# Small matmuls in column and row tiles, two thirds of an inverse transform, wider loads and a delayed output projection in an attention and FFT-gate kernel

## The chip, the cores and the metric

The kernel runs on one core of one Trainium2 chip. TensorE (PE) multiplies matrices into PSUM, VectorE (DVE) and ScalarE (ACT) do the elementwise work, GpSimd (POOL) adds a few tensors and starts most loads, and SyncE (SP) starts the stores. The metric is the time of one execution on the device in microseconds (us). "Span" is the part of it that the profile covers, about 2 us less. "Clock" is the mean share of full speed that TensorE was granted. Each run has a state, fast or slow; only fast runs are compared here.

## The reference, cut to what matters

```python
kv  = einsum('bhsd,bhse->bhde', k, v)        # 8 batches, 8 heads, 576 positions, 64 per head
o   = einsum('bhsd,bhde->bhse', q, kv)
o   = o / sqrt(mean(o*o, -1) + 1e-6) * g_norm
x   = o.transpose(0, 2, 1, 3).reshape(8, 576, 512)
x1, x2, x3 = split(x @ w_proj, 3, axis=-1)   # 512 -> 3 * 512
y   = x1 * irfft(rfft(x2, axis=1) * rfft(filter_fft, axis=0)) * x3   # along the 576 positions
out = y @ w_out                              # float32, 8 x 576 x 512
```

## The kernel before

Everything is held with channels on the 128 partitions and positions in the free dimension, until the x2 projection turns it. The transform over 576 positions is split into three groups of frequencies (those divisible by three, and the rest), so that x is first folded: with thirds x_0, x_1, x_2 it makes `rr = x_0 + x_1 + x_2` and `ab = (x_0 - x_2, x_1 - x_2)`. A batch's attention is computed between the stages of the batch before it, so that TensorE always has something to do.

```python
def att_x(b, j):                  # x = o * rstd, four times per batch
    ...
    bc = ps_tile("ps_bc")
    for h in range(2):            # spread rstd of each head over its 64 partitions
        nc.tensor.matmul(bc[:, h, 0:TH], ind_bc[:, j], s['rstd'][:, h], start=True, stop=True)
    nc.vector.tensor_mul(out=s['x'][:, j].rearrange("p (a b) -> p a b", a=2), in0=bc[:, :, 0:TH],
                         in1=s['o'][:, j].rearrange("p (a b) -> p a b", a=2))

def inv(b, dc):                   # all three thirds of the inverse transform
    ...
    for g in range(2, 6):
        nc.tensor.matmul(ip[:, 0:2, 0:SB], Y[:, g, d_], IV[:, g, 0:2 * SB].rearrange("p (a b) -> p a b", a=2), ...)
        nc.tensor.matmul(ip[:, 2, 0:SB], Y[:, g, d_], IV[:, g, 2 * SB:S], ...)
    nc.vector.tensor_add(out=u, in0=ip[:, 0:3, 0:SB], in1=st[b]['cs'][:, dc].to_broadcast([P, 3, SB]))
    nc.vector.tensor_mul(out=st[b]['yg'][:, dc], in0=u.rearrange("p a b -> p (a b)"), in1=g13[:, dc])

for b in range(B):
    proj2(b); kv(b + 1); qtr(b + 1); fft(b)
    load_kv(b + 2); load_q(b + 2)
    for dc in range(4):
        proj13(b, dc); att_o(b + 1, dc)
    invc(b)
    att_r(b + 1)                  # row sums and rstd
    for dc in range(4):
        inv(b, dc); att_x(b + 1, dc)
    fold(b + 1)
    outp(b)                       # output projection
# cut: the tests whether there is a next batch
```

The whole kernel:

## Time and profile before

| | before |
|---|---|
| time, median of 4 runs | 299.94 us (299.25 to 300.9) |
| span of the profiled run | 297.9 us, of which 44.6 before the first x2 projection and 29.9 after the start of the last |
| steady batch, start to start of the x2 projection | 31.9 us |
| granted clock in the steady batches | 1.00 |

TensorE is busy 87% of the span, its clock is granted in full in all slices after the prologue's, and it carries two thirds of the chain: it is the bottleneck. The table of stretches shows two steady batches; its columns are the window with its length, then busy us of PE, of PE's weight loads, of DVE, ACT and POOL, each with its count, then the granted clock, the share of the DMA engines, and GB/s.

```profile
108.50:140.40 31.90, 30.61 (x221) 18.68 (x223) 18.93 (x26) 15.17 (x24) 14.63 (x14) 1.00 0.86 94
140.40:172.30 31.90, 30.61 (x221) 18.65 (x223) 18.94 (x26) 15.16 (x24) 14.63 (x14) 1.00 0.85 94
```

Of 31.9 us TensorE works 30.61 and DVE 18.94. The last lines come from the chain that ended last, through the second half of the second batch: start, us, and what.

```profile
...
159.52 0.65 ACT sq L213
...
162.13 0.69 ACT rstd L226
...
162.87 0.40 PE ps_bc L234 x2
...
172.33 0.75 PE ps_x L286 x3
```

From 159.52 to 162.82 the chain is on ScalarE, from the square to rstd. TensorE isn't idle for that long: its timeline shows a wait of 0.56 us for rstd, before the broadcasts at 162.87.

### The profile page before, as it was taken

How to read it: one execution, taken by the hardware profiler on the slowest of the kernel's cores; microseconds unless marked ns; L12 is line 12 of the kernel's file. 1: busy time of each engine (PE TensorE's matmuls, PEld its weight loads, DVE VectorE, ACT ScalarE, POOL GpSimd, SP SyncE). 2: the span in 40 equal slices, each digit the busy share in tenths (PEclk: the TensorE clock that was granted, in tenths of full speed). 3: DMA queues.
4: the chain of work that ended last, by engine and by line, in shares of the span. 5: the costliest groups of instructions: out<-in, count | busy, mean ns of one | idle time of the engine just before them, and what ended most of it. 6: DMA issues, size and time to landing. Idle time of an engine off the chain costs nothing.

```text
span 297.9 us, 4540 instructions
## 1 busy us (share of the span) xinstructions
PE 260.5 (87%) x1816; PEld 158.6 (53%) x1833; DVE 175.0 (59%) x272; ACT 131.6 (44%) x197; POOL 124.2 (42%) x131
## 2 busy tenths in 40 slices
PE   0128699999999999999999999999999999999992
PEld 0027346664567436754666455744775367644760
DVE  7993431939184745657383909382756547482760
ACT  1135435380637243753457073815274336614313
POOL 8874568890099006920395019800240006000600
PEclk9999779999999999999999999999999999999999
DMA  5999999999499639990699049934000220004004
GB/s 34 151 189 206 172 126 152 112 104 71 161 87 112 42 134 79 124 64 27 150 144 78 2 158 115 105 21 161 0 3 0 81 80 0 3 0 158 2 0 158
DMA packets 95415, 26.58 MB, mean 89 GB/s; under 512 B 79970, under 2 KB 90786, under 8 KB 95394
## 3 DMA queue, kind: packets, MB, share of 16 engines
q0 software_dynamic: 90272, 16.85, 69.3%
q1 hardware_dynamic: 5122, 9.44, 8.9%
q8 instruction: 14, 0.23, 0.3%
q14 instruction: 7, 0.06, 0.1%
HBM read 33.69 MB, written 9.44 MB: 145 GB/s over the span
## 4 chain that ended last, share of the span: by engine, by line
PE 66%; DVE 19%; ACT 10%; issue 4%; ACTq 0%; DVEq 0%
PE ps_x L319 17%; PE ps_out L359 12%; PE ps_x L286 12%; PE ps_inv L343 6%; DVE tpw L302 5%; PE ps_bc L234 4%; DVE qT L203 3%; DVE tpw L303 3%; PE ps_kv L186 3%; PE ps_inv L345 2%; ACT osb L214 2%; PE ps_h L262 2%; ACT sq L213 2%; PE ps_qT L202 2%; PE ps_o L212 2%
## 5 line engine op out<-in xcount | busy, mean ns | idle before, releaser
L319 PE MATMUL ps_x<-x,wp 128*128 128x288 bf16 x512 | 67.5, 286 | 4.4 <-DVE tpw L303 4.4
L304 POOL TENSOR_TENSOR Y<-tpw 97x1024 bf16<-97x1024 f32 (+1 forms) x16 | 38.0, 2381 | 74.8 <-DVE tpw L303 74.8
L319 PEld LDWEIGHTS <-wp 128*128 128x128 bf16 x512 | 50.0, 98 | 19.7 <-issue 5.7
L107 POOL DMA_DIRECT2D kb<-in_k_dram x32 | 28.5, 903 | 73.3 <-PE ps_kv L187 67.3
L361 ACT COPY ot<-ps_out 128x1024 f32<-128x1024 f32 (+1 forms) x24 | 20.0, 867 | 63.7 <-PE ps_out L359 63.1
L203 DVE COPY qT<-ps_qT 128x1152 bf16<-128x1152 bf16 x16 | 11.5, 753 | 52.3 <-PE ps_qT L202 52.3
L325 DVE TENSOR_TENSOR g<-ps_x,x 128x576 bf16<-128x576 f32 x32 | 24.0, 754 | 25.7 <-PE ps_x L319 25.7
L359 PE MATMUL ps_out<-wo,yg 128*128 128x512 bf16 (+1 forms) x152 | 38.2, 383 | 0.4
L323 ACT CAST x<-ps_x 128x576 bf16<-128x576 f32 x32 | 20.4, 639 | 39.7 <-PE ps_x L319 39.7
L115 POOL DMA_DIRECT2D qb<-in_q_dram x40 | 34.0, 879 | 2.1 <-DMA wo<-in_moe_w_out_dram 1.8
L347 DVE TENSOR_TENSOR u<-ps_inv,cs 128x576 bf16<-128x576 f32 x32 | 24.0, 753 | 17.0 <-PE ps_inv L345 17.0
L343 PE MATMUL ps_inv<-IV,Y 128*128 128x384 bf16 x128 | 34.0, 328 | 0.0
L345 PE MATMUL ps_inv<-IV,Y 128*128 128x192 bf16 x128 | 31.4, 246 | 0.0
L235 DVE TENSOR_TENSOR x<-ps_bc,osb 128x576 bf16<-128x576 f32 x32 | 23.7, 749 | 7.1 <-PE ps_bc L234 6.2
L213 ACT ACTIVATE sq<-ps_o 128x576 bf16<-128x576 f32 x32 | 20.9, 652 | 15.4 <-PE ps_o L212 15.4
L359 PEld LDWEIGHTS <-yg 128*128 128x128 bf16 (+1 forms) x160 | 14.0, 100 | 23.9 <-issue 8.4
L288 ACT CAST x<-ps_x 128x1024 bf16<-128x1024 f32 (+1 forms) x24 | 20.1, 872 | 11.2 <-PE ps_x L286 11.2
L214 ACT ACTIVATE osb<-ps_o,g_col 128x576 bf16<-128x576 f32 x32 | 23.6, 738 | 0.0
L302 DVE TENSOR_TENSOR tpw<-ps_X,HH 97x1024 f32<-97x1024 f32 (+1 forms) x16 | 19.5, 1219 | 6.8 <-PE ps_X L300 6.3
L286 PE MATMUL ps_x<-wp,ab 128*128 128x512 bf16 x96 | 22.0, 379 | 0.0
L173 PE MATMUL ps_ft<-ident,IV 128*128 128x128 bf16 (+1 forms) x25 | 3.7, 306 | 18.9 <-ACT IV L163 18.3
L343 PEld LDWEIGHTS <-Y 128*128 128x128 bf16 x128 | 12.5, 97 | 13.1 <-issue 6.7
(91 smaller groups left out, 355.0 us busy)
## 6 DMA issues: line engine op xcount, KB each, us to landing
out_dram<-ot SPq DMA_DIRECT2D x16, 512.0 KB, 3.1
kb<-in_k_dram POOLq DMA_DIRECT2D x32, 128.0 KB, 4.6
vb<-in_v_dram POOLq DMA_DIRECT2D x8, 512.0 KB, 6.8
qb<-in_q_dram POOLq DMA_DIRECT2D x32, 128.0 KB, 5.8
wp<-in_moe_w_proj_dram POOLq DMA_DIRECT2D x3, 512.0 KB, 10.5
out_dram<-ot SPq DMA_DIRECT2D x8, 128.0 KB, 3.1
kt<-in_k_dram POOLq DMA_DIRECT2D x8, 64.0 KB, 4.0
vt<-in_v_dram POOLq DMA_DIRECT2D x8, 64.0 KB, 5.8
```

The lines of the kernel that those rows point to most:

```text
L107: nc.gpsimd.dma_start(out=kb[i][:, c], in_=src4(k, c * D, [1, D]))
L115: nc.gpsimd.dma_start(out=qb[b % 2][:n, c], in_=q[b, :, c * P:c * P + n, :].transpose([1, 0, 2]))
L213: nc.scalar.activation(out=s['sq'][:, j].rearrange("p (a b) -> p a b", a=2), in_=op[:, :, 0:TH], func=AF.Square)
L214: nc.scalar.activation(out=s['o'][:, j].rearrange("p (a b) -> p a b", a=2), in_=op[:, :, 0:TH], func=AF.Copy, scale=g_col)
L286: nc.tensor.matmul(pp[:, cc], t[:, j, o * P:(o + 1) * P], wp[:, j, DM:2 * DM], start=(j == 0), stop=(j == NDC - 1))
L302: nc.vector.tensor_mul(out=t_[:n, 0], in0=xp[:n], in1=HH[:n, g, 1:3])
L304: nc.gpsimd.tensor_add(out=Y[:n, 2 * g:2 * g + 2], in0=t_[:n, :, 0], in1=t_[:n, :, 1])
L319: nc.tensor.matmul(pp[:, h, 0:TH], w_, x[:, j, h * TH:(h + 1) * TH], start=(j == 0), stop=(j == NDC - 1))
L325: nc.vector.tensor_mul(out=st[b]['g13'][:, dc].rearrange("p (a b) -> p a b", a=2), in0=pp[:, :, 0:TH], in1=x1)
L343: nc.tensor.matmul(ip[:, 0:2, 0:SB], Y[:, g, d_], IV[:, g, 0:2 * SB].rearrange("p (a b) -> p a b", a=2), start=(g == 2), stop=(g == 5))
L345: nc.tensor.matmul(ip[:, 2, 0:SB], Y[:, g, d_], IV[:, g, 2 * SB:S], start=(g == 2), stop=(g == 5))
L359: nc.tensor.matmul(pp[:m, cc], yg[:, dc, c * P:c * P + m], wo[:, dc], start=(dc == 0), stop=(dc == NDC - 1))
```

## The change

The change wants to take work off TensorE, and waits out of its way:

- k^T v, the q transposes, the row sums, and the tails of the x2 and output projections have half-width or narrower outputs. They are put side by side in column tiles, two or four matmuls on the array at once: in the trace of before the 20 column-tiled filter matmuls of 512 columns follow each other at 0.114 us, full ones at 0.22. The broadcasts have short contractions and go in row tiles: eight take 0.45 us on the chain of the changed kernel, where two took 0.40 before.
- The three thirds of that part of the inverse which comes from frequencies not divisible by three sum to zero. So only two thirds of it are computed, and DVE makes the last from them.
- k is loaded in pieces of 1 KB, as v was before, and q in pieces of 2304 bytes (nine positions of one head side by side, in float32), both instead of 256 bytes. In q, position 9t + c then lies at row t, and the transposes give the positions ordered by c, then t. Something must bring them back into order, and the x multiply does it while it writes.
- The filter is folded as x is; three passes instead of six make the tables.
- The output projection of a batch runs in the next batch, between the row sums and the broadcasts.

The diff is cut to its core:

```diff
-            nc.gpsimd.dma_start(out=qb[b % 2][:n, c], in_=q[b, :, c * P:c * P + n, :].transpose([1, 0, 2]))
+            nc.gpsimd.dma_start(out=qb[b % 2][64 * g:64 * g + 64],
+                in_=bass.AP(tensor=q.tensor, offset=..., ap=[[NR * D, 64], [S * D, 4], [1, NR * D]]))   # NR = 9
 ... # kv: pairs of heads in column tiles
+                    nc.tensor.matmul(kvp[64 * hp:64 * hp + 64, 0, j * D:(j + 1) * D], kk, vv, ...)
 ... # att_x
-        nc.vector.tensor_mul(out=s['x'][:, j].rearrange("p (a b) -> p a b", a=2), in0=bc[:, :, 0:TH],
-                             in1=s['o'][:, j].rearrange("p (a b) -> p a b", a=2))
+            nc.vector.tensor_mul(out=s['x'][:, j].rearrange("p (h t c) -> p h c t", h=2, c=NR),
+                                 in0=bc[i][:, :, 0:TH].rearrange("p h (c t) -> p h c t", c=NR),
+                                 in1=s['o'][:, j].rearrange("p (h c t) -> p h c t", h=2, c=NR))
 ... # inv: 16 matmuls of 384 columns, and the last third from the first two
+                nc.tensor.matmul(ip[:, i, 0:2 * SB], Y[:, g, d_], IV[:, g, 0:2 * SB], ...)
+        nc.vector.tensor_add(out=u[:, :, 0:2], in0=pq, in1=cs.to_broadcast([P, 2, 2, SB]))
+        nc.vector.tensor_sub(out=w_, in0=cs[:, :, 0], in1=pq[:, :, 0])
+        nc.vector.tensor_sub(out=u[:, :, 2], in0=w_, in1=pq[:, :, 1])
 ... # the loop over the batches
-        invc(b)
         if nxt:
             att_r(b + 1)
-        for dc in range(NDC):
-            inv(b, dc)
-            if nxt:
-                att_x(b + 1, dc)
+        if b:
+            outp(b - 1)
         if nxt:
+            att_x(b + 1, 0)
+            att_x(b + 1, 1)
             fold(b + 1)
-        outp(b)
+        invc(b)
+        for dp in range(2):
+            inv(b, dp)
+    outp(B - 1)
```

In the new x multiply, the innermost index of the output, t, moves by nine elements of bf16: every element is written 18 bytes after the one before it.

## The prediction

> **What bounds the kernel now.** The page shows a 297.9 us span with PE busy 87%, DVE 59%, ACT 44%, POOL 42%. The table of stretches shows a steady batch of 31.9 us holding 30.6 us of PE, 18.9 of DVE and 15.2 of ACT. Starts in the PE timeline give each stage's cost per batch: x2 projection 4.42 us, k^T v 1.11, q transposes 1.12, transform 2.8, x1/x3 projection 7.84, attention product 0.98, row sums 1.08, broadcasts 1.4, inverse 3.93 plus 0.66, output projection 4.39: about 29.8 us. The other 2.1 us is waits: 0.63 for the spectrum multiplies, 0.56 for rstd. Before the loop, 44.7 us pass: six DVE table passes until about 22 us, an ACT-bound attention stage to 33.5, filter matmuls to 44.7, some at 0.43 us each on a slow clock.
>
> **What changes per batch, on PE.** Inverse: 16 matmuls of 384 columns at 0.163 us instead of 384+192 at 0.246: -1.3. Output tail, shared by two batches: -0.5. Tail of the folded x2 projection, in halves: -0.4. Row sums, four column tiles: about -0.5. Broadcasts in row tiles: about -0.8. That column tiles overlap is already shown: the 20 half-width filter matmuls of 512 columns took 2.28 us, 0.114 each, against 0.22 for full ones. k^T v becomes 40 matmuls of 64 columns and the transposes 36; [...] weight loads last 98 ns at 128 columns, 125 at 97, 110 at 64. I estimate 3.1 us for both stages, from 2.2: +0.9. Sum: PE about 27.2 us.
>
> **On DVE.** Rebuilding the third third costs about +0.8 us of busy time, the split q copies +0.3. DVE rises to about 20 us. The x multiplies now write at an 18-byte step; I expect them to stay near 0.75 us.
>
> **Critical path.** Output projection one batch behind hides the rstd wait. But x multiplies and fold (about 4.7 us on DVE) now stand before the next x2 projection, covered by 3.3 us of inverse: a new wait of about 0.5-0.9 us for the folded x. Broadcasts wait about 0.5 us for PSUM. The wait before the x1/x3 projection stays, 0.5-1 us. So about 2 us of waits stay, and DVE is almost co-critical. Batch: about 29.2 us, not 27.2; saved over the loop, some 19 us.
>
> **Prologue.** Three table passes instead of six (-8 us), 1 KB instead of 256 B reads, 22 instead of 40 filter matmuls, DVE sharing the first attention stage. DVE must wait for the filter load before the first q copies, so I take -10 us: first x2 projection near 34-35 us. The end grows by about 3.5 us (one more output projection), which batch 0 loses.
>
> **Predicted time: 271 us, 8 in 10 within 260 to 284.** Chances: faster 0.94, within 2% 0.04, slower 0.02.
>
> **Right or wrong is shown by:** steady batch 28.5-30 us in the stretches; inverse near 2.6 us; k^T v plus transposes 2.5-3.5 us; the x2 projection waiting on DVE's fold; x multiplies near 0.75 us; first x2 projection at 33-37 us.
>
> **What would make it wrong.** Narrow weight loads not overlapping: +1.5 us a batch. Stretched x multiplies [...]: up to +2.5 us a batch. A late filter load: +5 us. Fewer waits than I count: -1.5 us a batch.

Two passages are cut from this text. 29.8 us of TensorE's stages, less 1.3, 0.5, 0.4, 0.5 and 0.8, plus 0.9, is 27.2. But the +0.9 (3.1 from the measured 2.2) is only the author's estimate, set beside three measured weight-load times, the -0.8 for row tiles is an estimate too (the trace of before has none), and the "up to +2.5 us", outside the sum, has no measured duration behind it.

## More of the kernel before

Lines of the page of the kernel before follow: busy times of the engines with their shares of the span, TensorE's granted clock in tenths in 40 slices of the span, the engines' shares of the chain that ended last, and one group of instructions (line, engine, operation, tiles, shapes, count, then busy us and mean ns of one, then idle time before them).

```profile
PE 260.5 (87%) x1816; PEld 158.6 (53%) x1833; DVE 175.0 (59%) x272; ACT 131.6 (44%) x197; POOL 124.2 (42%) x131
...
PEclk9999779999999999999999999999999999999999
...
PE 66%; DVE 19%; ACT 10%; issue 4%; ACTq 0%; DVEq 0%
...
L235 DVE TENSOR_TENSOR x<-ps_bc,osb 128x576 bf16<-128x576 f32 x32 | 23.7, 749 | 7.1 <-PE ps_bc L234 6.2
...
```

The x multiplies of line 235 last 749 ns each, and they write in order.

## The result

| | before | after |
|---|---|---|
| time, median | 299.94 us | 341.81 us (338.87 to 343.08, 4 runs) |
| ratio | | 1.138 (1.130 to 1.146) |
| steady batch | 31.9 us | 35.7 to 38.7 us |
| clock, whole span | 0.99 | 0.89 |

A ratio is the mean time of one kernel's fast runs over that of the other's of the same rounds, so it is not quite the ratio of the medians. The changed kernel is 14% slower, where 10% faster was predicted. The page of the changed kernel, with the same kinds of lines as before:

```profile
PE 253.1 (75%) x1942; PEld 139.5 (41%) x1965; DVE 240.3 (71%) x283; ACT 133.9 (39%) x197; POOL 78.0 (23%) x80
...
PEclk9997879957997799975998799959995799779998
...
PE 56%; DVE 31%; issue 7%; DMA 3%; ACT 2%; ACTq 0%; SPq 0%; DVEq 0%
DVE x L267 21%; PE ps_x L377 18%; PE ps_out L425 8%; PE ps_x L344 8%; PE ps_X L358 6%; PE ps_x L332 3%; DMA fc<-in_moe_filter_fft_dram 3%; PE ps_qT L223 3%; DVE tpw L361 2%; PE ps_x L336 2%; PE ps_o L237 2%; PE ps_kv L208 2%; PE ps_X L365 2%; DVE x L278 1%; DVE rr L279 1%
...
L267 DVE TENSOR_TENSOR x<-ps_bc,osb 128x576 bf16<-128x576 f32 x32 | 82.2, 2848 | 29.7 <-PE ps_bc L264 29.7
...
L402 PE MATMUL ps_inv<-IV,Y 128*128 128x384 bf16 x128 | 35.8, 460 | 9.6 <-DVE x L267 9.6
...
L332 PE MATMUL ps_x<-wp,rr 128*128 128x512 bf16 x25 | 10.7, 501 | 19.9 <-DVE rr L279 18.9
...
L390 PE MATMUL ps_c<-IV,Y 97*128 97x192 bf16 x64 | 9.0, 301 | 13.7 <-DVE x L267 13.7
```

Line 267 is the x multiply. Its mean is 2848 ns where it was 749, and it alone has 21% of the chain; DVE has 31%, from 19%. TensorE has less work (253.1 us, from 260.5), although many of its slices now run at a reduced clock. The first part of the inverse (line 390) waits 13.7 us in all for the x multiplies, the rest (line 402) another 9.6, and the x2 projection of line 332 waits 18.9 us for the fold behind them. In the table of stretches two batches look so:

```profile
153.80:192.50 38.70, 31.92 (x234) 16.76 (x237) 27.73 (x29) 14.84 (x22) 9.12 (x8) 0.83 0.43 74
192.50:229.20 36.70, 30.31 (x242) 16.68 (x245) 27.67 (x29) 15.40 (x23) 9.11 (x8) 0.91 0.48 85
```

A batch is now 37 to 39 us long, DVE works 27.7 us in it, and the clock is 0.83 to 0.91. The chain through the end of one batch and the start of the next shows where DVE stands:

```profile
...
65.67 0.45 PE ps_bc L264 x8
66.12 0.13 DVE x L267
66.26 2.16 issue
68.42 7.98 DVE x L267 x3
...
77.77 0.56 DVE rr L279
...
78.37 0.61 PE ps_x L332
...
```

From the end of the broadcasts at 66.1 to the x2 projection at 78.37, nothing on the chain is TensorE's: four x multiplies, then the fold (the 2.16 us of "issue" are still the first multiply, by DVE's timeline). The last three multiplies take 7.98 us, 2.66 us each from start to start. The inverse, which was to cover them, has to wait for them itself, as lines 390 and 402 of the page say. By the code, the four broadcasts hold all four buffers of the PSUM pool until the multiplies have read them. The granted clock in this stretch, in the table of stretches again:

```profile
66.00:68.80 2.80, 0.11 (x4) 0.10 (x1) 2.69 (x2) 0.00 (x0) 0.00 (x0) 0.83 0.00 0
68.80:71.40 2.60, 1.46 (x9) 1.16 (x9) 2.60 (x2) 0.80 (x1) 0.00 (x0) 0.50 0.03 6
71.40:75.80 4.40, 4.33 (x16) 1.91 (x15) 4.40 (x2) 0.00 (x0) 0.00 (x0) 0.63 0.00 0
```

Towards the end of 2.8 us with next to no work the clock falls to half (0.83 is the mean over them), and the inverse runs on it. In finer stretches the clock reads 1.00 until 67.5 us, 0.50 from 68.0 to 73.0, and 1.00 again from 75.0 to 75.8. TensorE wasn't idle throughout before the fall: a wait of 1.57 us for rstd, 0.45 us of broadcasts, then the gap; from 64.0 to 67.5 us it worked 0.53 us.

### The profile page after: what moved, and what is told of

Same layout as the page of the kernel before. It is cut to its first block, busy times and chain, and to the rows that moved or that the text cites. A ratio compares the mean times of both kernels' runs of the same rounds, so it can differ in the third digit from the quotient of the medians.

```text
span 339.3 us, 4726 instructions
## 1 busy us (share of the span) xinstructions
PE 253.1 (75%) x1942; PEld 139.5 (41%) x1965; DVE 240.3 (71%) x283; ACT 133.9 (39%) x197; POOL 78.0 (23%) x80
## 4 chain that ended last, share of the span: by engine, by line
PE 56%; DVE 31%; issue 7%; DMA 3%; ACT 2%; ACTq 0%; SPq 0%; DVEq 0%
DVE x L267 21%; PE ps_x L377 18%; PE ps_out L425 8%; PE ps_x L344 8%; PE ps_X L358 6%; PE ps_x L332 3%; DMA fc<-in_moe_filter_fft_dram 3%; PE ps_qT L223 3%; DVE tpw L361 2%; PE ps_x L336 2%; PE ps_o L237 2%; PE ps_kv L208 2%; PE ps_X L365 2%; DVE x L278 1%; DVE rr L279 1%
## 5 line engine op out<-in xcount | busy, mean ns | idle before, releaser
L267 DVE TENSOR_TENSOR x<-ps_bc,osb 128x576 bf16<-128x576 f32 x32 | 82.2, 2848 | 29.7 <-PE ps_bc L264 29.7
L377 PE MATMUL ps_x<-x,wp 128*128 128x288 bf16 x512 | 67.5, 286 | 4.4 <-DVE tpw L361 4.4
L338 ACT CAST x<-ps_x 128x1024 bf16<-128x1024 f32 x8 | 8.1, 1012 | 73.4 <-PE ps_x L336 73.4
L425 PE MATMUL ps_out<-wo,yg 128*128 128x512 bf16 x120 | 29.8, 381 | 2.9 <-DVE yg L411 2.4
L344 PE MATMUL ps_x<-wp,ab 128*128 128x512 bf16 x96 | 27.2, 443 | 0.0
L226 DVE COPY qT<-ps_qT 128x512 bf16<-128x512 bf16 (+1 forms) x32 | 13.2, 452 | 18.1 <-PE ps_qT L223 17.8
L332 PE MATMUL ps_x<-wp,rr 128*128 128x512 bf16 x25 | 10.7, 501 | 19.9 <-DVE rr L279 18.9
L433 ACT COPY ot<-ps_out 128x1024 f32<-128x1024 f32 x16 | 16.1, 1006 | 13.7 <-PE ps_out L425 13.7
L360 DVE TENSOR_TENSOR tpw<-ps_X,HH 97x1024 f32<-97x1024 f32 (+1 forms) x16 | 19.5, 1219 | 1.8 <-PE ps_X L358 1.6
L361 DVE TENSOR_TENSOR tpw<-ps_X,HH 97x1024 f32<-97x1024 f32 (+1 forms) x16 | 19.4, 1213 | 0.0
L390 PE MATMUL ps_c<-IV,Y 97*128 97x192 bf16 x64 | 9.0, 301 | 13.7 <-DVE x L267 13.7
L407 DVE TENSOR_TENSOR u<-ps_inv,cs 128x768 bf16<-128x768 f32 x16 | 15.2, 950 | 4.7 <-PE ps_inv L402 4.7
L425 PEld LDWEIGHTS <-yg 128*128 128x128 bf16 x128 | 11.4, 98 | 17.2 <-DVE yg L411 3.3
```

Source lines behind the costliest of these rows:

```text
L267: nc.vector.tensor_mul(out=s['x'][:, j].rearrange("p (h t c) -> p h c t", h=2, c=NR), in0=bc[i][:, :, 0:TH].rearrange("p h (c t) -> p h c ...
L332: nc.tensor.matmul(pp[:, 0], rr[:, j, 0:P], wp[:, j, DM:2 * DM], start=(j == 0), stop=(j == NDC - 1))
L344: nc.tensor.matmul(pp[:, cc], ab[:, j, (c0 + cc) * P:(c0 + cc + 1) * P], wp[:, j, DM:2 * DM], start=(j == 0), stop=(j == NDC - 1))
L361: nc.vector.tensor_mul(out=t_[:n, 1], in0=xp[:n], in1=HH[:n, g, 0:2])
L377: nc.tensor.matmul(pp[:, h, 0:TH], w_, x[:, j, h * TH:(h + 1) * TH], start=(j == 0), stop=(j == NDC - 1))
L425: nc.tensor.matmul(pp[:, cc], yg[:, dc, c * P:(c + 1) * P], wo[:, dc], start=(dc == 0), stop=(dc == NDC - 1))
```

## The experiments

Three theories were on the table at first. A: the write at an 18-byte step is dear in itself. B: it isn't the step that is dear, but the short runs into which the pattern cuts 576 elements. C: the multiply is slowed by its neighbours, that is by other engines or by the place it now has in the batch. Later expectations name three more. D: the small tiles themselves cost as well. E: in the experiment on the output projection, the granted clock falls and makes batches longer. F: there, the waits alone do it, at full clock.

### Single operations by themselves (micro)

A kernel with no other work runs the multiply (576 columns, float32 from PSUM times bf16 from SBUF, to bf16) four times for each write pattern, and a few ScalarE, copy and matmul forms. Its output is wrong, which doesn't matter for the time.

```diff
+    for t in (d_one, d_two, d_three, d_four, d_six, d_eight, d_nine, d_sixteen):   # [P, 576, k], element 0 of k written
+        nc.vector.tensor_mul(out=t[:, :, 0]..., in0=src, in1=sb2)
+    # x_perm: the pattern of the change; f_perm: the same in float32
+    # x_runs: runs of 32, with gaps, written in order; x_read: read at a step, written in order
+    # a_one, a_perm, a_read: ScalarE copies in order, written at the step, read at the step
+    # c_one, c_perm: DVE copy of bf16 in PSUM, in order and written at the step
+    # m_one, m_step: matmuls of 288 columns, moving operand in order and at a step of 64 bytes
```

> A kernel that only measures single operations (its result is wrong on purpose); each operation runs four times on 576 elements of 128 partitions. Theory A (the write step alone): the multiply takes 0.75 us when it writes side by side, and in the pattern of the change, 18 bytes from element to element, about 2.7 to 2.9 us with no other engine at work; it grows with the step and is full from some step between 2 and 9 elements on; runs of 32 side by side with gaps between them stay near 0.75 us. Theory B (the short runs and the many dimensions of the pattern): the runs of 32 with gaps are as slow as the pattern of the change, and a plain step of 9 is near 0.75. Theory C (neighbours: GpSimd, matmuls or ScalarE at the same memory): the pattern of the change takes 0.75 us here. Open beforehand, for a repair: what a stepped read costs the matmul, ScalarE and the vector engine.

The groups of instructions of this kernel, by shape (line, engine, operation, tiles, shapes, count, busy us and mean ns):

```profile
L92 ACT CAST a_perm<-pa 128x576 bf16<-128x576 f32 x4 | 11.0, 2751 | 0.1
L64 DVE TENSOR_TENSOR d_eight<-ps,sb 128x576 bf16<-128x576 f32 x4 | 10.9, 2735 | 0.1
L70 DVE TENSOR_TENSOR x_perm<-ps,sb 128x576 bf16<-128x576 f32 x4 | 10.9, 2726 | 0.1
...
L64 DVE TENSOR_TENSOR d_four<-ps,sb 128x576 bf16<-128x576 f32 x4 | 6.5, 1625 | 0.0
L70 DVE TENSOR_TENSOR f_perm<-ps,sb 128x576 f32<-128x576 f32 x4 | 4.9, 1233 | 0.1
...
L64 DVE TENSOR_TENSOR d_two<-ps,sb 128x576 bf16<-128x576 f32 x4 | 3.2, 800 | 0.0
L76 DVE TENSOR_TENSOR x_runs<-ps,sb 128x576 bf16<-128x576 f32 x4 | 3.0, 753 | 0.1
L64 DVE TENSOR_TENSOR d_one<-ps,sb 128x576 bf16<-128x576 f32 x4 | 2.9, 737 | 0.1
L94 ACT CAST a_read<-pa 128x576 bf16<-128x576 f32 x4 | 2.9, 730 | 0.1
...
```

The pattern of the change takes 2726 ns alone on the chip, as in the kernel, so C falls. Runs of 32 written in order take 753 ns, so B falls. A stands: from step to step the time rises as 737 ns (1 element), 800 (2), 1196 (3), 1625 (4), 2078 (6), 2735 (8), 2722 (9), 2612 (16). ScalarE pays the same for such a write (2751 against 639 ns), and a DVE copy from PSUM too (2758 against 444). Reading at a step from PSUM costs ScalarE nothing that shows: three of its four copies took 639 or 640 ns and one 1004, which makes the mean 730. DVE, which read both inputs at a step, took 1112. For TensorE a step in the moving operand is dear too: 40 matmuls took about 19 us instead of 7.4. By their starts in the trace, the matmuls in order followed each other at 0.24 us until 7.1 us and at 0.12 after that (the trace's record of the clock begins only at 7.0 us), those at a step at 0.49 throughout, with a granted clock of 1.00 (9 to 12 us) as with one of 0.50 (15 to 29 us).

### The x multiply written in order (x_inorder)

This is the changed kernel with two letters swapped. x comes out in the wrong order, so the result is wrong; everything else is as in the change.

```diff
-            nc.vector.tensor_mul(out=s['x'][:, j].rearrange("p (h t c) -> p h c t", h=2, c=NR),
+            nc.vector.tensor_mul(out=s['x'][:, j].rearrange("p (h c t) -> p h c t", h=2, c=NR),
```

> The changed kernel with one edit: the multiply that makes x writes in the order of its inputs, so x comes out with its rows permuted and the result is wrong on purpose; all else, matmuls and waits, is as in the change. Theory A: x multiplies fall from 2.85 us to 0.75, a steady batch from about 37 us to 29 (28 to 30.5), the clock goes back over 0.97, first x2 projection near 35 us, total about 268 us (260 to 278), what the prediction said for the whole. Theory D (the small tiles themselves cost as well: [...]slow weight loads, a colder clock): total stays over 285 us.

It took 275.34 us, ratio 0.920 (0.917 to 0.924). The one line of code is worth 66.5 us. From the page, the x multiply:

```profile
...
L267 DVE TENSOR_TENSOR x<-ps_bc,osb 128x576 bf16<-128x576 f32 x32 | 22.0, 749 | 29.9 <-PE ps_bc L264 29.9
...
```

Two steady batches in the table of stretches:

```profile
93.90:123.10 29.20, 27.63 (x242) 15.98 (x245) 20.16 (x29) 15.40 (x23) 9.12 (x8) 1.00 0.60 107
123.10:151.30 28.20, 26.44 (x234) 15.47 (x237) 20.15 (x29) 14.84 (x22) 9.12 (x8) 1.00 0.60 101
```

And in the chain, two of the attention matmuls and the x multiplies of one batch:

```profile
...
109.87 0.24 PE ps_o L237 x2
...
117.55 0.39 PE ps_bc L264 x4
117.94 0.75 DVE x L267
...
119.27 1.42 DVE x L267 x2
...
```

The x multiplies are back at 749 ns, all four of a batch are done 2.8 us after the first one starts, and the clock is 1.00. Batches of 28.2 and 29.2 us alternate, since the tail of the output projection runs for two batches together. The prediction had said 29.2 us. From the first x multiply to the next x2 projection 4.7 us pass (117.93 to 122.67), where the changed kernel needs 12.3 (66.11 to 78.37). So what the change does on TensorE works as predicted, the step accounts for the loss, and D, which expected over 285 us here, falls.

### The step alone in the kernel before (before_xstride)

The reverse test puts only the stepped write into the kernel before; the result is wrong.

```diff
-        nc.vector.tensor_mul(out=s['x'][:, j].rearrange("p (a b) -> p a b", a=2), in0=bc[:, :, 0:TH],
-                             in1=s['o'][:, j].rearrange("p (a b) -> p a b", a=2))
+        nc.vector.tensor_mul(out=s['x'][:, j].rearrange("p (h t c) -> p h c t", h=2, c=9),
+                             in0=bc[:, :, 0:TH].rearrange("p h (c t) -> p h c t", c=9),
+                             in1=s['o'][:, j].rearrange("p (h c t) -> p h c t", h=2, c=9))
```

> The kernel before with only the write of x in the pattern of the change (wrong result on purpose). Theory A: x multiplies from 0.75 to about 2.7 to 2.9 us, the inverse stage, where they alternate with the multiplies of y, becomes bound by the vector engine and grows by about 8 us a batch; the total goes to 350 to 375 us, which is more than the changed kernel's 342. Theory D: below 320 us, the rest being due to the small tiles.

Two runs took 364.18 us in the median, ratio 1.215 (1.207 to 1.223), at a clock of 0.88. The chain of one batch:

```profile
...
152.13 2.71 DVE x L235
154.84 0.28 DVE yg L349
155.13 0.66 DVE u L348
155.79 2.60 DVE x L235
...
```

The four multiplies alternate with the two DVE instructions of the inverse, and the output projection must wait for the last of all. The step costs this kernel 64.6 us (299.62 us without it in the same rounds), nearly the same as the changed one. So it needs nothing else of the change to do its harm. Part of the loss comes through the clock (0.88 here): after the multiplies, 11 matmuls of the output projection take 4.46 us on the chain, where 18 took 4.39 before.

### Other ways to put the positions in order

The positions must be brought into order somewhere. Four kernels do it in other places, and all of them give correct results.

**In the matmul (pe_unpermute).** The attention product reads q^T at a step of 64 bytes.

```diff
-        st[b]['qT'] = qT.rearrange("p j h c t -> p j h (c t)")
+        st[b]['qT'] = qT.rearrange("p j h c t -> p j h t c")
 ... # x multiply in order, as before
```

> A repair with a right result: the attention matmul reads the transposed q with 64 bytes from element to element, so its output comes in natural order and the x multiply writes side by side. Theory A: x multiplies 0.75 us; if the matmul reads a step at full rate, total as x_inorder, near 268 us; if at half rate, 8 matmuls of 288 a batch cost 0.12 us more each, about 1 us a batch, near 276 us. Theory D: over 285 us.

It took 294.69 us, ratio 0.985 (0.982 to 0.988). Its chain shows two attention matmuls as

```profile
...
118.00 0.97 PE ps_o L237 x2
...
```

so 0.49 us each, against 0.12 in the chain of x_inorder above. Eight of them per batch take about 2.9 us more, and the kernel takes 19.4 us more than x_inorder, 2.4 per batch: the moving operand of a matmul can't be read at that step for nothing either. Both cases of the expectation (268 and 276 us) were too low, since the matmul ran at a quarter of the rate, not at half.

**In the tables (perm).** The whole batch stays in another order (inside each third, c first); the tables, the filter's loads and the stores follow it. The diff touches the iota of the tables, the loads of q and of the filter, and cuts each store of 256 rows into four.

```diff
-    nc.gpsimd.iota(tvi, pattern=[[1, S]], base=0, channel_multiplier=0)
+    nc.gpsimd.iota(tvi.rearrange("p (m c t) -> p m c t", m=3, c=3), pattern=[[SB, 3], [1, 3], [3, 64]], ...)
 ...
-                nc.sync.dma_start(out=out[b, c0 * P:(c0 + 2) * P, :].rearrange("(c p) d -> p c d", p=P), in_=ot)
+                for kk in range(4):
+                    put(b, 2 * c0 + kk, ot[64 * (kk % 2):64 * (kk % 2) + 64, kk // 2])
```

> A repair with a right result and no permuting at run time: q is loaded so that the order of rows (64 groups of 3) stays within each third, the tables and the filter are made in the same order, and the output rows are put in place by the stores (nine of 64 rows of 2 KB a batch instead of two and a half). x multiply side by side. Theory A: steady batch as x_inorder, total within 1% of x_inorder, at most 2 us more at the end for the split stores. Theory D: over 285 us.

It took 279.6 us, ratio 0.936 (0.933 to 0.939). From the second batch on its batches are those of x_inorder. The 4 us it loses, more than was expected, lie in the first batch (31.2 us instead of 29.1, after a start 1.0 us earlier) and after the last x2 projection, 39.4 us instead of 36.0. There ScalarE's last copy ends 31.8 us after the start of that projection in both kernels, so what is longer is the split stores.

**In ScalarE's read (act_unpermute).** The square and the scaled copy after the attention product already read PSUM and write SBUF. They now read at a step and write in order.

```diff
+        on = op[:, :, 0:TH].rearrange("p h (c t) -> p h t c", c=NR)
-        nc.scalar.activation(out=s['sq'][:, j].rearrange("p (a b) -> p a b", a=2), in_=op[:, :, 0:TH], func=AF.Square)
+        nc.scalar.activation(out=s['sq'][:, j].rearrange("p (h t c) -> p h t c", h=2, c=NR), in_=on, func=AF.Square)
 ... # the scaled copy likewise; the x multiply in order, as before
```

> A repair of three lines with a right result: ScalarE, which reads the attention output from PSUM anyway, reads it at the step and writes its two results in natural order; the x multiply then writes side by side, and q loads and stores are as in the change. The small measurement showed ScalarE reading PSUM at the step in 0.64 us, as fast as in order. Theory A: total within 1% of x_inorder (275 us), about 24 us below before; the first batch, where the vector engine does half of this, loses about 1.5 us. Theory D (something else of the change costs): does not apply any more below 285 us.

It took 275.07 us, ratio 0.9175 (0.914 to 0.9205). The square takes 650 ns and the scaled copy 734, as they did before (652 and 738): the reordering costs nothing there.

**Not at all (q_rows).** q is loaded and transposed as in the kernel before, in pieces of 256 bytes; everything else is the change.

```diff
-            nc.gpsimd.dma_start(out=qb[b % 2][64 * g:64 * g + 64], in_=bass.AP(..., ap=[[NR * D, 64], [S * D, 4], [1, NR * D]]))
+            nc.gpsimd.dma_start(out=qb[b % 2][:n, c], in_=q[b, :, c * P:c * P + n, :].transpose([1, 0, 2]))
```

> The changed kernel with q loaded and transposed as before (256 bytes a row, full transposes, two copies), which needs no permuting at all; right result; k and v keep their 1 KB loads. Theory A: x multiply 0.75 us, steady batch within 0.5 us of act_unpermute, as DMA is not on the chain in the loop; the prologue loses 0 to 2 us for a later q. Total 272 to 278 us: so the wide q load, which brought the step, gained nothing. Rival: the loads matter, total over 280 us.

It took 274.69 us, ratio 0.918 (0.914 to 0.922), the same as act_unpermute within the runs' spread. So the wide loads of q, for which the positions were permuted at all, gained nothing that can be measured. What is compared is each way as a whole: q_rows has the old transposes and copies of q too, and the 1 KB loads of k and v stay in both. The steady batches take 28.0 and 29.0 us by turns, those of act_unpermute 28.2 and 29.2.

### What single parts of the change are worth

Two parts were undone one at a time, starting from act_unpermute.

**All three thirds of the inverse (au_full_inverse).**

```diff
-                nc.tensor.matmul(ip[:, i, 0:2 * SB], Y[:, g, d_], IV[:, g, 0:2 * SB], ...)
+                nc.tensor.matmul(ip[:, 0:2, 0:SB], Y[:, g, d_], IV[:, g, 0:2 * SB].rearrange("p (a b) -> p a b", a=2), ...)
+                nc.tensor.matmul(ip[:, 2, 0:SB], Y[:, g, d_], IV[:, g, 2 * SB:S], ...)
 ... # u and yg as before
```

> act_unpermute with the inverse of before: all three thirds by matmuls (24 of 576 columns' worth a batch) and no rebuilding on the vector engine. My account of the change: matmul time up by 1.3 us a batch, vector engine down by about 0.8; as the batch is tied by both in turn I expect 1 us a batch longer, total plus 6 to 10 us. Rival: the vector engine is the tighter one there (the x2 projection waits for the fold, not for matmuls), then the total stays within 3 us or falls.

It took 278.85 us, ratio 0.931 (0.928 to 0.935). The two-thirds inverse is worth 3.8 us, less than was expected: 0.77 us per steady batch instead of the 1.3 us of matmul time that it saves. The chains say why. With the long inverse, the chain runs from the inverse straight into the next x2 projection, and the fold is done by then. With the short one, it runs through the x multiplies and the fold: part of what TensorE saves uncovers a wait for DVE. After the last x2 projection the short inverse even loses 1.5 us (34.4 us against 32.9).

**The output projection in its own batch (au_outp_now, and once more as outp_now_again).**

```diff
-        if b:
-            outp(b - 1)
-            del st[b - 1]
 ...
-    outp(B - 1)
+        outp(b)
```

> act_unpermute with the output projection back at the end of its own batch instead of one batch later. My account: the projection no longer covers the rstd wait and stands behind the last multiplies of y, so 2 to 4 us a batch more, total plus 12 to 25 us. Rival: it only moves the waits (then it covers the fold before the next x2 projection, which waits about 1 us now), and the total stays within 5 us.

Its two fast runs took 327.06 and 330.43 us, ratio 1.097 (1.0885 to 1.105), a larger loss than was expected. The other two were slow, 332.96 and 443.99 us. The profiled run is that of 443.99 us: a clock of 0.57, with 0.50 or 0.56 granted from about 27 us to the end; the others ran at 0.88 to 0.91, and no run here says why. So the same kernel was run again.

> The same kernel as au_outp_now, for a profile of an execution that is not slow (that one's profile had a granted clock of 0.57). Fast executions took 327 to 333 us, far more than my account's 287 to 300. Theory E (clock): the output projection, once it doesn't stand between the row sums and the broadcasts, leaves the matmul engine idle for stretches of several us, the granted clock falls, and matmuls run at half speed for long parts: then the clock reads near 0.91, and batches differ from each other by several us. Theory F (chain): the waits alone add 7 us to each batch, at full clock, all batches alike.

This time it took 331.91 us, ratio 1.109 (1.103 to 1.115), in a fast run. Batches last 35.3 to 40.0 us. In TensorE's timeline between two stages, with the idle time before each piece and what ended it, one sees:

```profile
...
168.80 0.43 PE L265 MATMUL ps_bc<-rstd,ind_bc 32*128 32x288 bf16 x8 [1.57 <-ACT rstd L255]
170.05 1.44 PE L390 MATMUL ps_c<-IV,Y 97*128 97x192 bf16 x8 [0.81 <-DVE x L268]
171.28 5.27 PE L402 MATMUL ps_inv<-IV,Y 128*128 128x384 bf16 x16
...
```

And in the table of stretches around it:

```profile
166.00:170.00 4.00, 1.15 (x17) 0.51 (x17) 1.47 (x3) 2.60 (x4) 0.00 (x0) 0.94 0.00 1
170.00:173.00 3.00, 2.95 (x14) 1.99 (x14) 2.97 (x5) 0.80 (x1) 0.00 (x0) 0.50 0.00 0
173.00:177.00 4.00, 3.54 (x12) 1.35 (x10) 2.75 (x5) 0.00 (x0) 0.00 (x0) 0.58 0.00 0
```

With the row sums done and the output projection no longer there, TensorE has nothing to run while ScalarE makes rstd and DVE the first x. It works 1.15 us of 4. Then the clock is granted at 0.50, and the inverse takes 5.27 us instead of the 2.76 of act_unpermute. After it comes another wait, for the gated y, and again a half clock (1.29 us of work from 177 to 181 us, then a clock of 0.50 from 181 to 185). Both explanations, E and F, have their part: by the chain of this batch the waits (rstd and ScalarE's chain before it 2.7 us, the x multiply 0.8, the gated y 4.1) make some 7.6 us. Set against the same stages at full clock, the inverse and the output projection lost some 6 us (an estimate from the two chains). The sum is more than the 10.8 us by which this batch (40.0 us) exceeds one of act_unpermute (29.2), since some work is done inside the waits and act_unpermute has waits of its own.

This experiment is no full return to the kernel before, in which a part of the inverse stands between the row sums and the first broadcast (it fills ScalarE's 3.3 us there, as its chain shows). It says what the delayed output projection is worth in the order of the changed kernel, not in that of the old one.

### The wait for the filter (au_filter)

In the prologue, DVE's first q copies stand behind one instruction of the filter's fold that waits for the filter's load. The scratch buffer of the fold shares its memory with the output tiles. Here it has another buffer's memory, which was to let the order change.

```diff
-        t0 = work.tile([P, 2, DM], FP32, name="t0", tag="ot", bufs=3)
+        t0 = work.tile([P, 2, DM], FP32, name="t0", tag="qT")
```

> act_unpermute with the filter's scratch tile in the buffer of the transposed q, so that the vector engine can't fold the filter before the first q copies; right result. In act_unpermute the vector engine sits 6.7 us waiting for the filter load ahead of the first copies of q. Expected: first copies of q 2 to 4 us earlier, the first x2 projection 1 to 3 us earlier, total 272 to 274 us; if only another wait takes its place, 275.

It is a miss: 279.95 us, ratio 0.936 (0.932 to 0.940), about 5 us worse than act_unpermute. The first q copies do come 2.1 us earlier (20.39 us instead of 22.49), but another instruction of the fold now waits for the load, ahead of the first scaled copy, and the first x2 projection starts at 41.9 us instead of 37.5. The steady batches are the same. How to take this wait away stays open.

### Which writes are dear (micro2)

A second kernel of single multiplies writes bf16 in runs of r elements, one run per 64 bytes, and float32 in single elements at several steps; it too is wrong.

```diff
+    for t, r in ((r_one, 1), (r_two, 2), (r_four, 4), (r_eight, 8), (r_sixteen, 16)):
+        nc.vector.tensor_mul(out=t[:, :, 0:r].rearrange("p (a n) r -> p a n r", a=2), ...)
+    for t in (f_one, f_two, f_four, f_eight, f_sixteen):      # float32, [P, 576, k], element 0 of k written
+        nc.vector.tensor_mul(out=ap(t), in0=src, in1=sb2)
```

> Measures single operations again (wrong result on purpose): the multiply of 576 elements, writing bf16 in runs of 1, 2, 4, 8, 16 elements, one run every 64 bytes, and f32 one element every 1, 2, 4, 8, 16 elements. If the cost is per separate place written (each time a write doesn't go on next to the last): runs of 2 cost half of runs of 1, about 1.4 to 1.6 us, runs of 4 about 0.8, and f32 with gaps costs as much as bf16 with gaps, 2.7 us. If it is for writes of less than 4 bytes [...]: runs of 2 are near 1.2 us or less, and f32 with gaps stays at 1.2 us at most at every step, as the 36-byte step of the first measurement did (1.18).

The groups of instructions:

```profile
L61 DVE TENSOR_TENSOR r_one<-ps,sb 128x576 bf16<-128x576 f32 x4 | 10.6, 2638 | 0.1
...
L71 DVE TENSOR_TENSOR f_sixteen<-ps,sb 128x576 f32<-128x576 f32 x4 | 4.5, 1120 | 0.1
L61 DVE TENSOR_TENSOR r_two<-ps,sb 128x576 bf16<-128x576 f32 x4 | 3.2, 806 | 0.1
...
```

Single bf16 elements, far apart, take 2638 ns for 576; pairs take 806, and longer runs 754 or 755. Float32 elements far apart take 1120 to 1189 ns, and every second one still 754. So the expectation's first case (each separate place costs) fails, and the numbers of its second (writes of less than four bytes cost) hold.

What the two kernels of single operations show together is this. Of the steps tried, those from 16 bytes on differ little: bf16 takes 2735 ns at 8 elements, 2722 at 9 and 2612 at 16; float32 takes 1165 ns at 4, 1189 at 8 and 1120 at 16. At the 16-byte step that makes 4.7 ns per element in bf16 (2735 over 576) and 2.0 in float32 (1165 over 576); pairs of bf16, 64 bytes apart, come to 2.8 per pair at most (806 over 288). So here a lone two-byte write cost more than a lone write of four bytes. The step in bytes alone doesn't decide: 8 bytes cost 1625 ns in bf16 and 754 in float32. What the memory does with a two-byte write isn't shown by any run.

## Why the prediction was wrong

- **The step that failed** is, in the prediction's words: "The x multiplies now write at an 18-byte step; I expect them to stay near 0.75 us." They took 2.85 us by the records, 2.66 from start to start. The prediction had named the risk, but had put it at "up to +2.5 us a batch". The measured cost is 7.5 us per batch, and all of it is on the chain, since the x2 projection needs the fold and the fold needs all four multiplies: from the first x multiply to the next x2 projection 12.3 us pass in each of the seven batches, and 4.7 in those of x_inorder after the first. Taking the step away brought 66.5 us (341.81 less 275.34). By the starts of the x2 projections, that is 6.3 us before the first, and 8.5 us in each of the seven periods (37.3 against 28.8 in the mean). What goes beyond the 7.5 us fits the reduced clock after the gaps, which the steady batches of x_inorder don't have: the x2 projection that follows takes 5.6 us (78.37 to 84.01) at a clock of 0.72, against 4.2 at 1.00 (93.47 to 97.69 in x_inorder).
- **The reason for the mis-sizing** is that the trace of before had no stepped bf16 write, and the estimate took a small penalty for something that no duration backed. 32 instructions on the chain each cost 3.5 times what was assumed.
- **Steady batch on TensorE: right.** The prediction said 29.2 us, with 27.2 of work; x_inorder showed 28.7 in the mean (28.2 and 29.2 by turns), with 26.4 and 27.6 of work. In the loop of x_inorder the trace shows column-tiled weight loads of 64 columns at 108 to 118 ns in the mean and of 32 columns at 94, against 98 for full ones. (The 125 ns at 97 columns, which the prediction lists beside them, belong to loads that aren't column-tiled.) And they overlap: 40 matmuls of k^T v took 0.75 us (before, 20 took 1.11), and 36 transposes 1.13. Their sum of 1.9 us is well below the 3.1 that was estimated, and below the 2.5 to 3.5 that was named as a test; so this term was mis-sized too, to the good.
- **DVE: right but for the x multiplies.** It worked 20.2 us per batch in x_inorder, as predicted, and the fold was the new wait before the x2 projection, as predicted (0.25 and 0.50 us by turns; 0.5 to 0.9 had been said).
- **Prologue: nearly right.** The first x2 projection began at 36.2 us in x_inorder (predicted 34 to 35).
- **The end and the first batch: wrong by about 6 us together, partly made good by the steady batches.** After the start of the last x2 projection, 36.0 us passed, 6.1 more than before; 3.5 was predicted. The prediction further assumed that the first batch, which has no output projection, would be shorter by the 3.5 us. It was not: it took 29.1 us, at a clock of 0.88. Its chain shows the wait for ScalarE's 2.7 us and then an inverse of 4.8 us instead of 2.76; the same stage takes 5.0 us in the first batch of act_unpermute, at a clock of 0.50 to 0.56, and 5.27 in outp_now_again, at 0.50 to 0.58. The batch lost by idle TensorE what it had saved in work.
- **The wide loads of q: no gain.** q_rows showed that they can be left out without a loss (274.69 against 275.07 us). They were the only reason for the permuted order, so the part that cost 66 us had bought nothing.

Without the stepped write the prediction's 271 us would have been 275, inside its range.

The best two of the correct versions are act_unpermute at 275.07 us and q_rows at 274.69 us, 8% faster than the kernel before. The repair is three lines in the first and the old load in the second.

What was not tried apart: what the row tiles, the column tiles, the 1 KB loads of k, the folded filter and the fewer table passes each bring by themselves. Only sums are seen: the TensorE work of a batch, 27.0 us in the mean instead of 30.6, and the first x2 projection at 36.2 us instead of 44.6.

## What to carry to other kernels

When a layout change needs a permutation, look for the instruction that can do it on its PSUM read while it writes SBUF in order: here ScalarE did it for nothing (650 ns against 652 in order), while the stepped bf16 write cost the multiply 3.5 to 3.8 times the time and ScalarE's copy 4.3 times, and a stepped moving operand cost four times at full clock. If an estimate rests on an operation in a form that the trace doesn't hold, measure that form alone first; one kernel of single operations would have shown it. When work is moved away from a place, ask what TensorE does there instead, because such gaps (2.8 us with 0.11 us of work, 4 us with 1.15) were paid twice here, once as a wait and once as a half clock (0.50 granted in both).
